# A first block ahead of the first states, a tick ahead of two scalings, and a sixth buffer, in a retention and Mish kernel on one core

## The chip, the core and the metric

The kernel runs on one core of a Trainium2 chip. The metric is the device time of one execution in microseconds (us); the times of several executions are given as a median with the lowest and the highest. Engines are named as in the profile: PE is TensorE, PEld its weight loads, DVE VectorE, ACT ScalarE, POOL GpSimd, SP SyncE (which only issues DMAs here).

## The reference

Batch 8, 8 heads, 576 positions, head size 64; the MLP has 512 columns and 2048 inner ones. In short:

```python
scores = q @ k.transpose(0, 1, 3, 2) / np.sqrt(64)
gamma  = 1 - 2.0 ** (-5 - np.arange(8))
rel    = pos[:, None] - pos[None, :]
ret    = scores * np.where(rel >= 0, gamma[:, None, None] ** rel, 0)   # causal decay, no softmax
x      = (ret @ v).transpose(0, 2, 1, 3).reshape(8 * 576, 512)
h      = x @ w_in                                                      # 4608 x 2048
out    = (h * np.tanh(log1p(exp(h)))) @ w_out                          # Mish, then 4608 x 512
```

## The kernel before

**Chunks and tiles.** The 4608 rows are cut into 36 chunks of 128. The first eight are the first 128 positions of the eight batches; the others hold positions 128 to 511 of each batch in three chunks, and the last 64 positions of two batches together. Four chunks make a tile of 512 rows, nine tiles in all (t = 0 to 8). For a tile, retention gives `xT` (512 columns by 512 rows), `g1(t, f)` makes block f of 16 of the inner layer (four 128x512 matmuls into one of two PSUM banks named hp, L568 or in halves L573, and a Mish activation on ACT into `gT`, L584), and the down projection multiplies `gT` by `w_out`.

**Retention in chunks.** A chunk's q and k are scaled on DVE (`step_p`, L341, two instructions, named P), its v by the decay (`step_v`, L348, named V: on DVE for chunks under 16, on POOL from 16 on). q and k are transposed (`step_t`: on PE for chunks under 16, by SP's DMA after that). A `visit(n)` for the pair n, n+1 adds the products of k and v of the next pair to the running states (L426), makes the outputs of its own pair from masked scores (L482) and from earlier states (L498), the scores of the next pair (L380), and after that DVE's mask product (`step_m`, L386). The scaled v of a chunk is in a buffer of the pool `tok`, which has five; a buffer is free when the matmuls of its chunk's visit have read it.

**The order.** The schedule is written by hand: every engine runs its instructions in the order in which the Python text gives them, and a semaphore wait holds up all that stands behind it on that engine. Three stretches of it matter here.

1. *Tile 0's down projection with tile 1's retention* (16 steps, `steps` at L860). Letters name tile 1's pieces: O is the output product of a batch's first chunk (`f_out`, its copy into `xT` at L251, half on DVE and half on ACT), F is `f_state` (L257, DVE), which scales v of one batch for the states that the first chunks leave. The down projection's four row blocks end in two hp banks, a bank ops and a bank st, and each is copied to `res` (L638) and stored by SP.
2. *Tile 1's sixteen blocks* (the loop over u at L893). `FIRST` places the first states in it: `first_states(of, what)` (L289, small matmuls, 64 rows and 64 columns) for tile `of`, row half `what`, into the banks st and ops; after the second half ACT copies both banks (L300). "turn" transposes tile 1's k (L264) and copies it, half on DVE and half on ACT (L270). `ps`, `vs` and `ts_` place the scalings and transposes of chunks 8 to 13.
3. *The later tiles* (the loop at L951), where n is the pair that is visited and w the step of eight in its half tile. In tile 2's second half (n = 14, i = 8 and 9) the loop asks for V of chunks 16 and 17. `tick` (L946) is a copy of one column of the newest `gT` block to `held` on POOL (L949), which makes POOL's queue wait for that activation; from i = 9 of tile 2 on it stands ahead of every load and every pair of scalings on POOL.

POOL also issues the loads of q, k and v (L325 and L329). At the visits of chunks 18, 20, 26, 30 and 32 the matmuls of the whole visit are in one step (w = 6), while V of the pair four chunks on is asked for at w = 3 (behind 32 there is none left).

Of the kernel before, what the change touches and what calls it, by code (L numbers as in the profile page):

```python
# [16 lines left out]
def kernel(  # L17
# [18 lines left out]
    nc = tc.nc  # L36
# [9 lines left out]
    NPE = 16  # L46
# [16 lines left out]
    wpool = ctx.enter_context(tc.tile_pool(name="weights", bufs=1))  # L63
    first = ctx.enter_context(tc.tile_pool(name="first", bufs=1))
    io = ctx.enter_context(tc.tile_pool(name="io", bufs=PF))
    tok = ctx.enter_context(tc.tile_pool(name="tok", bufs=5))
    tr = ctx.enter_context(tc.tile_pool(name="tr", bufs=4))
    xp = ctx.enter_context(tc.tile_pool(name="xp", bufs=2))
    gp = ctx.enter_context(tc.tile_pool(name="gp", bufs=2))
# [101 lines left out]
    def f_mix(g, i):  # L171

        name = ("qb", "kb")[i]
        fst[1][name, "mix", g] = room[3][:, ts(i, 1024)].rearrange("p (r x d) -> p r x d", r=8, x=2)
        nc.vector.tensor_copy(fst[1][name, "mix", g].rearrange("p r x d -> p x r d"),
                              fst[1][name][:, ds(2 * g, 2), :].rearrange("p x (r d) -> p x r d", r=8))
# [76 lines left out]
    def f_state(t, b, engine=nc.gpsimd):  # L253

        n = 4 * t + b
        v0s[n] = room[(6, 3)[t]][:, ts(b, H * D)].rearrange("p (h d) -> p h d", h=H)
        engine.tensor_tensor(v0s[n], v0[n], gv[:, 0, :].unsqueeze(2).to_broadcast([P, H, D]), op=OP.mult)  # L257

    def f_k0(t):

        tp = ps_sc.tile([P, 2, H, P], BF16, name="sc")
        for g in range(2):
            for h in range(H):
                nc.tensor.transpose(tp[:, g, h, :], fst[t]["kb", g][:, h, :], ident)  # L264
        return tp

    def f_k0_copy(t, tp, copies):
        for g in range(2):
            pair = first.tile([P, 2, H, D], BF16, name="k0", bufs=2)
            copies[g](pair.rearrange("p x h d -> p h x d"), tp[:, g].rearrange("p h (x d) -> p h x d", x=2))  # L270
            for x in range(2):
                k0[4 * t + 2 * g + x] = pair[:, x]
# [24 lines left out]
    def first_states_copy(t, copy):  # L297
        for i in range(2):
            pair = first.tile([P, 2, NP, 64], F32, name="s0", bufs=4)
            copy(pair, s0_banks[t][i])  # L300
            for x in range(2):
                s0[4 * t + 2 * i + x] = pair[:, x]
# [81 lines left out]
    def step_m(n):  # L384
        sm = tr.tile([P, 2, 2, NP, 64], BF16, name="sm", bufs=2)
        nc.vector.tensor_tensor(  # L386
            sm.rearrange("p e x n i -> p (e x n) i"), live[n]["sc"].rearrange("p e x n i -> p (e x n) i"),
            mask.unsqueeze(1).to_broadcast([P, 4 * NP, 64]), op=OP.mult)
        live[n]["sm"] = sm
# [405 lines left out]
    def att(n, steps):  # L795
        if n >= n_chunks:
            return
        for step in steps:
            {"P": step_p, "V": step_v, "T": step_t}[step](n)
# [57 lines left out]
        g1(0, f)  # L857
    for i in range(2):
        f_mix(0, i)
    steps = {0: "T0", 3: "S0 C1", 9: "T1", 11: "S1", 12: "V0 V1 V2 V3", 13: "F0 F1", 14: "O0 O1 O2 O3", 15: "F2 F3"}  # L860
    for i in range(nF):
        for step in steps.get(i, "").split():
            n = int(step[1])
# [25 lines left out]
    ps = {0: 0, 4: 1, 8: 2, 11: 3, 17: 5}  # L889
    vs = {0: 0, 5: 1, 9: 2, 13: 3, 18: 4, 19: 5}  # L890
    ts_ = {3: 0, 7: 1, 12: 2, 14: 3, 19: 4, 21: 5}
    FIRST = {0: (0, 0), 1: (1, 0), 2: ("turn", 1), 5: (0, 1), 6: (1, 1)}
    for u in range(24):  # L893
        j, w = divmod(u, 4)
        halved[0] = 2 if u < 1 else 0
        if u in FIRST:
            what, of = FIRST[u]
            if what == "turn":
                f_k0_copy(of, f_k0(of), (dve, act))
            else:  # L900
                first_states(of, what)
                if what:
                    first_states_copy(of, act)
        if u in ps:
            att(N0 + ps[u], "P")
        if u == 11:
            step_m(N0)
        if u in vs:
            att(N0 + vs[u], "V")
        if w == 0 and j > 0:  # L910
            if j < 5:
                load(N0 + j + 3)
            else:
                more_loads(N0 + j + PF)
        if u == 10:
            units = states(N0)
            units[0]()
            step_s(N0)
            units[1]()
            run(sums)  # L920
        elif u == 16:
            att(N0 + 4, "P")
            visit(N0, ((ps_o, "ops"), (ps_h, "hp")), (act, act))
            run(sums)
        elif u == 22:
            visit(N0 + 2, ((ps_h, "hp"), (ps_h, "hp")), (act, dve))
        if u == 20:
            stores(act)
        if u in (13, 20):
            run(casts, dve if u == 13 else act)  # L930
        if u in ts_:
            att(N0 + ts_[u], "T")
        stores()
        if u < nF:
            g1(1, u)
            flush()
        else:
            g2(1, u - nF)
# [7 lines left out]
    def tick(t, i):  # L946

        f = done.get(t, 0)
        nc.gpsimd.tensor_copy(held[:, i % 2:i % 2 + 1], gts[t][:, f, 0:1])  # L949

    for t in range(NS, nT):  # L951
        for i in range(nF):
            n, w = NCH * (t + 1) + i // 8 * 2, i % 8
            if w == (2 if t == NS else 0):
                run(casts, act)
            if t == NS and i == 0:
                halved[0] = 12
            for job in PLAN[i] if t > NS else ():
                if job[0] == "S":
                    g_sum(t - 1, int(job[1]))  # L960
            if t == NS:
                if w == 6:
                    visit(n, ((ps_h, "hp"), (ps_h, "hp")), (act, dve))
            elif n in WHOLE:
                if w == 6:
                    visit(n, ((ps_h, "hp"), (ps_h, "hp")), (act, act))
                elif w == 7:
                    run(sums)
            elif w == 2 and n < n_chunks:
                visit_first(n)  # L970
            elif w == 6 and n < n_chunks:
                visit_second(n, act)
            if w == 0:
                stores(act)
            if w == (3 if t > NS else 7 if n + 2 == NPE else 0) or w == 0 and n + 2 == NPE:
                run(sums)
            if w == 7 and n + 2 == NPE:
                stores(act)
            if w in (0, 1) and n + 2 < NPE:
                att(n + 2 + w, "P")  # L980
            if w == 1 and n + 4 == NPE:
                more_loads(n + 7)
            if w in ((4, 7) if n + 2 == NPE else (4, 5)) and n + 4 >= NPE:
                att(n + 4 + (w > 4), "P")
            if w in ((3, 4) if n + 2 < NPE else (0, 1)) and n <= NPE - 2:
                att(n + 2 + (w in (1, 4)), "V")
            if n + 2 >= NPE and w == (6 if n + 2 == NPE else 3) and n + 4 < n_chunks:
                tick(t, i)
                att(n + 4, "V")
                att(n + 5, "V")  # L990
            if t == NS and i in (3, 6, 10, 13):
                w_sum({3: 1, 6: 6, 10: 7, 13: 4}[i])

            if t == NS + 1 and i == 3:
                w_sum(3)
            if w == 7 and n + 4 == NPE:
                att(n + 5, "T")
            if w == (5 if n <= NPE - 2 else 7) and n + 4 >= NPE:
                att(n + 4, "T")
            if n + 2 >= NPE and w in PACED:  # L1000
                m, part = ((0, 2), (1, 2), (0, 0), (0, 1), (1, 0), (1, 1))[PACED.index(w)]
                if n + 6 + m < n_chunks:
                    tick(t, i)
                    load_part(n + 6 + m, part)
            if w == 5 and n + 4 < NPE:
                more_loads(n + w + 2)
            if w in (4, 5) and n + 2 < NPE:
                att(n - 2 + w, "T")
            if w == 0 and n == NPE or w == 7 and n >= NPE:
                att(n + (3 if w == 0 else 5), "T")  # L1010
            stores(act)


            if t == 2:
                if w == 6:
                    g2(1, 8 + i // 2)
                g1(t, i)
                if i % 2 and w != 7:
                    g2(1, 8 + i // 2)
            else:  # L1020
                if i == 15:
                    rest()
                jobs = (PLAN if n < n_chunks else ALONE)[i]
                for job in reversed(jobs) if n in WHOLE and w == 6 else jobs:
                    if job[0] == "g":
                        g1(t, int(job[1:]))
                    elif job[0] == "U":
                        unit(t - 1, int(job[1:]))
                if i == 8:
                    rest()  # L1030
# [31 lines left out]
```

## Time and profile before

| what | value |
|---|---|
| median of 3 runs | 294.47 us (294.01 to 295.0) |
| the profiled execution, its span | 293.21 us, 291.5 us |
| granted TensorE clock | 1.0 |
| busy time: PE, DVE, ACT, POOL | 282.3, 189.4, 155.3, 151.4 us |
| HBM | 36.70 MB read, 9.44 MB written, 158 GB/s over the span |

The profile is of one execution. Its times start at the span's start. A line such as `54.39 1.03 PE L568 MATMUL ... x4` of the timeline gives the start, the duration, the engine, the line of the kernel, the operation with its tiles and shapes, and how many were merged; brackets give the idle time of the engine before it and what ended that. A line of the waits gives who waited for whom, for how long in total, how often, and the longest.

### The profile page before, as it was taken

To read this page: it belongs to the slowest core of one execution; us is meant where nothing else is said; L and a number is where in the kernel's file an instruction comes from. 1 tells how busy PE (TensorE), PEld (TensorE's weight loads), DVE (VectorE), ACT (ScalarE), POOL (GpSimd) and SP (SyncE) were. 2 spreads that over 40 slices of the span, in tenths; PEclk is the share of its full clock that TensorE was granted. 3 is DMA by queue.
4 is the path that set the end of the run, shared out by engine and by line. 5 is a ranking of instruction groups with operands and counts; after the bars stand their busy time and mean duration, and the time that the engine had idled before them with its cause. 6 is when DMAs were issued, how large, how long until landed. Compare 5 with 4: busy or idle time off the path is not lost.

```text
span 291.5 us, 8716 instructions
## 1 busy us (share of the span) xinstructions
PE 282.3 (97%) x3788; PEld 186.2 (64%) x3788; DVE 189.4 (65%) x273; ACT 155.3 (53%) x269; POOL 151.4 (52%) x225
## 2 busy tenths in 40 slices
PE   7899999999998999999999999999999999999994
PEld 3566786555664556666756766666666766665783
DVE  4842449739699399786588767966786173523383
ACT  5656324876674564755464646554656556444320
POOL 8695842688792977567379875777430000000000
PEclk9999999999999999999999999999999999999999
DMA  7999999987999995959696996499826001201033
GB/s 156 206 206 205 205 237 231 290 210 161 236 261 176 162 199 122 179 157 168 197 187 177 187 236 159 146 179 218 183 86 127 12 2 73 74 0 72 22 104 94
DMA packets 41543, 45.91 MB, mean 158 GB/s; under 512 B 23841, under 2 KB 31265, under 8 KB 41505
## 3 DMA queue, kind: packets, MB, share of 16 engines
q0 software_dynamic: 14256, 30.15, 49.5%
q1 hardware_dynamic: 26656, 14.69, 24.0%
q8 instruction: 29, 0.48, 0.7%
q10 hardware_dynamic: 592, 0.52, 0.6%
q14 instruction: 10, 0.07, 0.1%
HBM read 36.70 MB, written 9.44 MB: 158 GB/s over the span
## 4 chain that ended last, share of the span: by engine, by line
PE 84%; DVE 6%; DMA 5%; POOL 2%; issue 1%; ACT 1%; POOLq 0%; ACTq 0%
PE hp L568 38%; PE ops L680 26%; PE hp L573 5%; DMA gT<-in_v_dram 3%; DVE qks L341 2%; DMA qkraw<-in_k_dram 2%; PE hp L680 2%; PE ops L568 2%; PE sc L426 2%; PE sc L380 1%; PE sc L759 1%; POOL gT L107 1%; PE ops L573 1%; PE st L573 1%; DVE sm L386 1%
## 5 line engine op out<-in xcount | busy, mean ns | idle before, releaser
L568 PE MATMUL hp<-xT,w_in_t 128*128 128x512 bf16 x534 | 129.9, 379 | 0.2 <-ACT gT L584 0.2
L584 ACT ACTIVATE gT<-hp 128x512 bf16<-128x512 f32 x144 | 86.1, 600 | 60.6 <-PE hp L568 58.5
L568 PEld LDWEIGHTS <-w_in_t 128*128 128x128 bf16 x534 | 50.9, 98 | 47.5 <-issue 1.6
L680 PEld LDWEIGHTS <-room 128*128 128x128 bf16 x528 | 51.3, 98 | 13.6 <-issue 0.8
L341 DVE TENSOR_TENSOR qks<-qkraw,gqk 128x512 bf16<-128x512 f32 x56 | 45.0, 854 | 4.9 <-issue 4.0
L671 DVE TENSOR_TENSOR room<-gT 128x2048 bf16<-128x2048 bf16 x35 | 42.2, 1229 | 0.8 <-ACT gT L584 0.8
L680 PE MATMUL ops<-room,room 128*128 128x256 bf16 x304 | 37.5, 273 | 0.5 <-ACT res L710 0.5
L949 POOL COPY held<-gT 128x1 bf16<-128x1 bf16 x57 | 19.4, 340 | 29.0 <-ACT gT L584 28.9
L348 POOL TENSOR_TENSOR vs<-vraw,gv 128x512 bf16<-128x512 f32 x20 | 26.2, 1319 | 11.7 <-PE hp L482 11.7
L386 DVE TENSOR_TENSOR sm<-sc,mask 128x1024 bf16<-128x1024 f32 x14 | 17.1, 1221 | 17.5 <-PE sc L380 10.8
L680 PEld LDWEIGHTS <-gT 128*128 128x128 bf16 x224 | 21.7, 98 | 6.2 <-issue 0.2
L680 PE MATMUL ops<-w_out_t,room 128*128 128x256 bf16 x192 | 22.9, 273 | 0.0
L325 POOL DMA_DIRECT2D vraw<-in_v_dram x24 | 21.3, 887 | 2.6 <-DMA w_out_t<-in_moe_w_out_dram 1.4
L325 POOL DMA_DIRECT2D qkraw<-in_q_dram x24 | 21.7, 904 | 1.7 <-issue 1.3
L325 POOL DMA_DIRECT2D qkraw<-in_k_dram x24 | 21.2, 883 | 0.0
L450 DVE TENSOR_TENSOR total<-sc,total 128x256 f32<-128x256 f32 x32 | 13.5, 423 | 3.6 <-PE sc L426 2.8
L680 PE MATMUL ops<-room,gT 128*128 128x256 bf16 x112 | 13.4, 273 | 0.0
L573 PEld LDWEIGHTS <-gT 128*128 128x128 bf16 x120 | 11.6, 98 | 2.4
L573 PE MATMUL hp<-xT,w_in_t 128*128 128x256 bf16 x84 | 12.6, 273 | 0.0
L680 PE MATMUL ops<-w_out_t,gT 128*128 128x256 bf16 x96 | 12.3, 273 | 0.0
L568 PE MATMUL ops<-w_out_t,gT 128*128 128x512 bf16 x46 | 12.1, 380 | 0.0
L712 DVE TENSOR_TENSOR res<-ops,res 128x512 f32<-128x512 f32 x6 | 4.2, 692 | 12.1 <-PE ops L680 12.1
(156 smaller groups left out, 348.6 us busy)
## 6 DMA issues: line engine op xcount, KB each, us to landing
out_dram<-res SPq DMA_DIRECT2D x29, 256.0 KB, 4.1
qkraw<-in_q_dram POOLq DMA_DIRECT2D x24, 256.0 KB, 6.0
qkraw<-in_k_dram POOLq DMA_DIRECT2D x24, 256.0 KB, 6.7
vraw<-in_v_dram POOLq DMA_DIRECT2D x24, 256.0 KB, 6.6
w_out_t<-in_moe_w_out_dram POOLq DMA_DIRECT2D x4, 512.0 KB, 11.1
w_in_t<-in_moe_w_in_dram POOLq DMA_DIRECT2D x3, 512.0 KB, 9.6
out_dram<-res SPq DMA_DIRECT2D x9, 128.0 KB, 2.5
gT<-in_k_dram POOLq DMA_DIRECT2D x8, 128.0 KB, 6.5
```

What stands on the lines that cost most here:

```text
L325: nc.gpsimd.dma_start(out=t, in_=src[b, :, ds(P * c, P), :].rearrange("h p d -> p h d"))
L341: nc.vector.tensor_tensor(slots[:, :, y], heads[:, :, y], factors[:, :, y].unsqueeze(3).to_broadcast([P, NP, 2, D]), op=OP.mult)
L348: engine.tensor_tensor(vs, live[n]["v"], gv[:, c, :].unsqueeze(2).to_broadcast([P, H, D]), op=OP.mult)
L386: nc.vector.tensor_tensor(sm.rearrange("p e x n i -> p (e x n) i"), live[n]["sc"].rearrange("p e x n i -> p (e x n) i"), mask.unsqueeze(1) ...
L426: nc.tensor.matmul(st[ds(64 * e, 64), j, x, p, :], lhsT=ks, rhs=vs, start=True, stop=True, skip_group_check=True)
L450: nc.vector.tensor_tensor(new[:, k], st[:, j, x], total[b], op=OP.add)
L568: nc.tensor.matmul(to, lhsT=w, rhs=x, start=first, stop=last)
L573: nc.tensor.matmul(to[:, ts(j, n)], lhsT=w, rhs=x[:, ts(j, n)], start=False, stop=False, skip_group_check=True)
L584: nc.scalar.activation(gts[t][:, f, :], hp, AX.Mish)
L671: engine.tensor_tensor(to, g_half(t, *a), g_half(t, *b), op=op_)
L680: nc.tensor.matmul(bank[:, half, :], lhsT=g[:, f, ts(half, P)], rhs=w[:, f, :], start=(f == 0 and half == 0 and not add), stop=(f == hF - ...
L949: nc.gpsimd.tensor_copy(held[:, i % 2:i % 2 + 1], gts[t][:, f, 0:1])
```

## The change

Three edits, in one file:

- In the u loop the first states of tile 0 and the turn of tile 1's k each move one step back (u = 1, 2, 3 in place of 0, 1, 2), so that block 0 of tile 1 stands first. The scalings F0 and F1 move from step 13 to step 15 of the stretch before, behind the O steps; F2 and F3 move from step 15 to u = 1 and u = 2, called directly.
- At tile 2, i = 8, a `tick` is put ahead of V of chunks 16 and 17. `done` is then 7: it is the block with index 7 of tile 2.
- The pool `tok` gets six buffers in place of five.

PE and DVE run the same instructions as before in another order, POOL one copy more; ACT runs the same as well, and SP's order is as before.

```diff
-    tok = ctx.enter_context(tc.tile_pool(name="tok", bufs=5))
+    tok = ctx.enter_context(tc.tile_pool(name="tok", bufs=6))
...
-    steps = {0: "T0", 3: "S0 C1", 9: "T1", 11: "S1", 12: "V0 V1 V2 V3", 13: "F0 F1", 14: "O0 O1 O2 O3", 15: "F2 F3"}
+    steps = {0: "T0", 3: "S0 C1", 9: "T1", 11: "S1", 12: "V0 V1 V2 V3", 14: "O0 O1 O2 O3", 15: "F0 F1"}
...
-    FIRST = {0: (0, 0), 1: (1, 0), 2: ("turn", 1), 5: (0, 1), 6: (1, 1)}
+    FIRST = {1: (0, 0), 2: (1, 0), 3: ("turn", 1), 5: (0, 1), 6: (1, 1)}
...
         if u in vs:
             att(N0 + vs[u], "V")
+        if u in (1, 2):
+            f_state(1, u + 1, nc.vector)
...
+            if w == 0 and n + 2 == NPE:
+                tick(t, i)
             if w in ((3, 4) if n + 2 < NPE else (0, 1)) and n <= NPE - 2:
                 att(n + 2 + (w in (1, 4)), "V")
```

## The prediction

> **What bounds the kernel now.** I read the page's busy table first, then TensorE's list of waits, then its timeline around each wait, then the timelines of VectorE, ScalarE and GpSimd at the same places.
>
> The page's first part:
> ```profile
> PE 282.3 (97%) x3788; PEld 186.2 (64%) x3788; DVE 189.4 (65%) x273; ACT 155.3 (53%) x269; POOL 151.4 (52%) x225
> ```
> TensorE (PE) is the bound, so only what makes PE wait can pay. The clock row is 9 in all forty slices. PE's waits (waited for: total, times, longest, in us):
> ```profile
> PE sc L426 <- DVE vs L348: 0.8, 1, 0.8
> PE st L289 <- ACT res L638: 0.7, 1, 0.7
> ...
> PE ops L680 <- ACT res L710: 0.5, 1, 0.5
> ...
> PE hp L568 <- ACT gT L584: 0.2, 1, 0.2
> ```
> Behind the first 17 us these four are all: no other entry lies there. In PE's timeline (start, duration, line, tiles, count, idle before):
> ```profile
> 48.48 0.38 PE L568 MATMUL st<-w_out_t,gT 128*128 128x512 bf16 x1
> 49.54 0.22 PE L289 MATMUL st<-room,k 64*64 64x64 bf16 x2 [0.68 <-ACT res L638]
> ...
> 54.39 1.03 PE L568 MATMUL hp<-xT,w_in_t 128*128 128x512 bf16 x4
> 55.57 1.02 PE L568 MATMUL hp<-xT,w_in_t 128*128 128x512 bf16 x4 [0.15 <-ACT gT L584]
> ...
> 87.27 1.03 PE L568 MATMUL ops<-w_out_t,gT 128*128 128x512 bf16 x4
> 89.05 0.32 PE L426 MATMUL sc<-vs,qks 64*64 64x64 bf16 x16 [0.75 <-DVE vs L348]
> ```
> Ends of matmuls are modelled, so I count starts. Eight 128x512 matmuls start 1.73 us apart from the next group (62.89 to 64.62), 0.216 each. The matmul of 48.48 is done with its turn at 48.70 and the next starts at 49.54: **stall A, 0.84 us**. In the same way 54.39 + 0.86 = 55.25, next at 55.57: **stall B, 0.32**. And 87.27 + 0.86 = 88.13, next at 89.05: **stall C, 0.92**. Without a wait, a change to the 64-row matmuls leaves 0.09 (50.62 + 0.22 = 50.84, next 50.93).
>
> Stall A is the first states: they write the banks st and ops, in which the first tile's last two row blocks lie until ScalarE (48.90 to 49.49) and VectorE (48.85 to 49.53) have copied them out. Stall C is the visit of chunk 12, which needs the scaled v of chunk 15. VectorE and GpSimd there:
> ```profile
> 85.42 1.53 DVE L341 TENSOR_TENSOR qks<-qkraw,gqk 128x512 bf16<-128x512 f32 x1
> 86.87 1.53 DVE L341 TENSOR_TENSOR qks<-qkraw,gqk 128x512 bf16<-128x512 f32 x1
> 88.32 0.68 DVE L348 TENSOR_TENSOR vs<-vraw,gv 128x512 bf16<-128x512 f32 x1
> ```
> ```profile
> 86.36 1.48 POOL L348 TENSOR_TENSOR vs<-vraw,gv 128x512 bf16<-128x512 f32 x1
> 89.61 1.50 POOL L348 TENSOR_TENSOR vs<-vraw,gv 128x512 bf16<-128x512 f32 x1 [1.76 <-PE hp L482]
> ```
> A scaling at L341 has a median of 0.68; these two take 1.53 each, the second while GpSimd scales v of chunk 16 (86.36). The 1.70 that they lose is what makes chunk 15's v late.
>
> **First edit, the block ahead of the states.** The same instructions run; only their order changes. PE goes from 48.70 straight into block 0 of tile 1. Its input xT must be there: ScalarE's half ends at 48.07; VectorE's half, today 47.72 to 48.94 behind two scalings (1.28), moves ahead of them and runs about 46.60 to 47.82. The two hp banks were copied out by 46.63. So the block fills 48.70 to 49.57 and hides the copies (VectorE's now 48.05 to 48.73, as its source ends at 47.99; ScalarE's unchanged to 49.49). The states follow at 49.66 with the 0.09 change: A falls from 0.84 to 0.09, gain 0.75.
>
> What is late next? The transposes of k (0.90) now end at 53.19, block 3 runs 53.64 to 54.50, block 4 to 55.36, the states of tile 1's row half to 55.87. ScalarE runs behind: VectorE's k copy 53.39 to 54.08, ScalarE's k copy (1.01, which today too starts when VectorE's ends) to 55.1, half a qkT copy (0.59, overlapping) to 55.6, block 3's activation to about 56.1. Block 5 needs that activation's bank, so it waits from 55.87 to about 56.15: stall B moves from block 4 to block 5 at nearly its size. Gain 0; bounds +0.32 (gone) and -0.7 (one more 1.01 copy ahead of the activation, less the 0.3 already counted). I take 0, because it is the same queue with the same copies.
>
> The four scalings of tile 1's v for the states (0.60 apart, 2.4 in all) move behind the xT copy; the last two end near 52.9, and VectorE has 0.74 idle today ahead of the k copy, so nothing waits for them. SP's queue keeps its order: the marker between the two row halves of the states stands behind two stores and is due at 50.95, as today at 50.93. No DMA moves.
>
> **Second edit, the tick ahead of chunks 16 and 17.** One more 128x1 copy on GpSimd (0.19 to 1.25 in the rows of L949) waits for block 7 of tile 2, whose activation starts at 93.13 and ends at 93.73. Both scalings, today at 86.36 and 89.61, then start near 94. Chunk 16's key scaling on VectorE falls from 2.98 to about 1.28, chunk 15's v is ready at 87.3, ahead of PE at 88.13: C falls from 0.92 to 0.09, gain 0.83. Only the second of the slowed scalings lies beside GpSimd's scaling in the rows; if the first one's 0.85 is something else, v is ready at 88.15, and the gain is still about 0.8. The other inputs of that visit are there: the last transposed chunk is copied by 87.77, block 5's bank is free at 88.25.
>
> Behind the waiting tick GpSimd holds the two scalings and the loads that today start at 95.29. The scalings take 1.04 (alone) to 1.50 (beside VectorE), so they end at 96.1 to 97.6; the next visit needs them at 100.79, 3 us later. The loads start 1.3 to 3 us later; the last of their group today is issued about 104.7, takes 4.5 to 5.7 to land, and is read behind 112.14 + 1.3. There is cover of 1 to 3 us; without it VectorE would be late by the rest, with the mask product of 116.66 behind it. I count nothing.
>
> **Third edit, the sixth buffer.** It removes no PE wait: PE waits for no scaled v but at C. It removes GpSimd's waits:
> ```profile
> its engine sat idle before it (us, times) until:
>   PE hp L482: 11.7, 5
> ```
> One is the 1.76 above; the rest are at the visits of chunks 18, 20, 26 and 30 (2.25, 3.76, 1.71, 2.25). There the second scaling of a pair will run right behind the first, beside VectorE's four key scalings, and the loads go out earlier by as much. Where two run together today (112.23) VectorE's four take 4.18, where one does 3.34 (125.63): 0.84 more. VectorE's idle time ahead of the next mask product is 1.06, 1.35, 0.51 and 1.04, so only the third is short, by 0.33, and 1.08 of idle follows there. I count 0.
>
> The Trainium skill, "SBUF — State Buffer", section "Who interferes with whom", speaks against this edit: a VectorE instruction with two SBUF inputs and a GpSimd one that reads SBUF shut each other out, the later one standing still for a whole instruction. By it a meeting costs a whole scaling, 1.04 in place of 0.84; then two more of the four idle times (1.06, 1.04) are used up to within 0.02 and the third is short by 0.53. The sum would stay, but I would give the third rival below 0.15 in place of 0.11.
>
> **Sum.** 0.75 + 0 + 0.83 = 1.58. The profiled execution took 293.21 (span 291.5, 1.7 around it): 291.6. It lies 1.26 under the median of 294.47, from which the same 1.6 gives **292.9**. All stages behind 90 us are PE-bound, with loads gated by activations, so the gain is carried to the end; the stall of 0.70 at 151.21 hangs on a chain that starts from PE and stays.
>
> **The rivals.** (1) *Only one stall goes.* Either ScalarE's queue makes B grow by what A gives (bound -0.7 above), or chunk 15's v still comes late. For: both have under 0.4 us of slack in my working. Against: each slack is positive. Time: 294.47 - 0.8 = 293.7.
> (2) *Nothing is left.* PE is at 97%, and both gains turn into waits further on, VectorE being held by landings: it waited 0.91 for one at 56.68. Against: chunk 17's key load, issued at 79.34 with a median of 6.1 to land, is there by 85.5, and VectorE wants it at 86.4 even when 0.8 early. Time: 294.5.
> (3) *Slower, by the sixth buffer.* At the four visits GpSimd holds VectorE for two scalings in a row. The longest key scaling in the rows is 2.09, 1.41 over the usual; two of these are 2.82, against 0.85 counted today, so 1.97 more at each, past the idle times by 0.91, 0.62, 1.46 and 0.93, 3.9 in all. If mask products and the copies behind them passed all of it on to PE: 294.47 - 1.6 + 3.9 = 296.8. It decides from 0.6 of PE loss per visit. Against: 2.09 is a single row, and 1.1 of idle follows behind most of these products.
>
> **How the numbers follow.** About 0.3% (0.9 us) is what a measurement of this kernel can tell from no change. Both stalls gone: 0.63, between 292.2 and 293.4 with B's bounds. Rival 1: 0.17, within 0.3%, though a part of it (0.03) reaches past. Rival 2: 0.09. Rival 3, with other ways to lose: 0.11. So faster 0.66, same 0.23, slower 0.11. The range takes in the first two and most of rival 2, down to B gone and the run's own spread of 0.5: 292.0 to 294.3.
>
> **What would show it.** Right: PE goes from the last st matmul to an hp matmul 0.22 later; no wait of L289 for L638; a wait of some 0.3 at block 5 in place of block 4; L426 waits no longer for L348; chunk 16's two key scalings take about 0.7 each (one may be 1.5); GpSimd's scalings stand behind a tick at about 92, with no wait for L482 anywhere. Wrong: a new PE wait of over 0.5 us behind ScalarE's k copy, at the visits of chunks 14, 18, 20, 26 or 30, or a wait of VectorE for a landing ahead of one of these.

## The result, and the profile after

The changed kernel takes 292.5 us (median; 291.89 to 292.89) against 294.47 (294.01 to 295.0), five executions of each: a ratio of 0.9935 with a 95% interval of 0.9916 to 0.9954, or 1.9 us less (1.35 to 2.5). A second measurement, made with the last experiments, gave 0.9927 (0.9908 to 0.9946). The forecast was 292.9. Comparisons leave out executions that took over 1.5% more than the fastest of the same kernel, and two profiles of such executions (303.6 us, the first edit alone; 297.4, the changed kernel with five buffers), which have further PE waits from 100 us on, are read up to 95 us only.

The profiled execution has a span of 290.7, only 0.8 less than before. The rest is lost at its start, where PE waits longer for first loads: 1.4 for q, against 0.6 before (the first line below), and 0.5 for the first weights, against nothing. So what stood at 48.48 before stands at 49.39. PE's list of waits (waited for: total, times, longest), the kernel before and then the changed one:
```profile
PE st L193 <- DMA gT<-in_q_dram: 0.6, 1, 0.6
```
```profile
PE st L193 <- DMA gT<-in_q_dram: 1.4, 2, 0.8
PE ops L164 <- DVE room L126: 1.3, 1, 1.3
PE ops L680 <- ACT res L710: 0.5, 1, 0.5
PE hp L568 <- DMA w_in_t<-in_moe_w_in_dram: 0.5, 1, 0.5
...
PE hp L568 <- ACT gT L584: 0.3, 1, 0.3
```
The waits for L638 (stall A) and for L348 (stall C) are gone; behind 22 us only L710 and L584 are left. So times are compared from the last st matmul of L568 on. PE's timeline at the places of the prediction:
```profile
49.39 0.38 PE L568 MATMUL st<-w_out_t,gT 128*128 128x512 bf16 x1
49.60 0.38 PE L568 MATMUL hp<-xT,w_in_t 128*128 128x512 bf16 x1
...
50.57 0.22 PE L289 MATMUL st<-room,k 64*64 64x64 bf16 x2
...
57.04 1.02 PE L568 MATMUL hp<-xT,w_in_t 128*128 128x512 bf16 x4 [0.27 <-ACT gT L584]
...
59.24 0.61 PE L360 MATMUL sc<-ident,qks 128*128 128x128 bf16 x8
...
87.40 1.03 PE L568 MATMUL ops<-w_out_t,gT 128*128 128x512 bf16 x4
88.36 0.32 PE L426 MATMUL sc<-vs,qks 64*64 64x64 bf16 x16
...
150.48 1.03 PE L680 MATMUL ops<-room,room 128*128 128x256 bf16 x8 [0.54 <-ACT res L710]
```
From the last st matmul to four landmarks:

| landmark | before | after | less |
|---|---|---|---|
| chunk 9's transposes (59.12, 59.24) | 10.64 | 9.85 | 0.79 |
| the visit of chunk 12 (89.05, 88.36) | 40.57 | 38.97 | 1.60 |
| the wait for L710 (151.21, 150.48) | 102.73 | 101.09 | 1.64 |
| end of the span (291.5, 290.7) | 243.0 | 241.3 | 1.7 |

The gain is made in two places, 0.79 and 0.81, and carried to the end. VectorE and GpSimd at the second one:
```profile
85.54 1.29 DVE L341 TENSOR_TENSOR qks<-qkraw,gqk 128x512 bf16<-128x512 f32 x2
86.74 0.69 DVE L348 TENSOR_TENSOR vs<-vraw,gv 128x512 bf16<-128x512 f32 x1
```
```profile
85.86 0.88 POOL L325 DMA_DIRECT2D vraw<-in_v_dram  x1
93.07 0.19 POOL L951 COPY held<-gT 128x1 bf16<-128x1 bf16 x1 [6.32 <-ACT gT L584]
93.21 3.02 POOL L348 TENSOR_TENSOR vs<-vraw,gv 128x512 bf16<-128x512 f32 x2
```
Chunk 16's two key scalings take 1.29 in place of 2.98, although GpSimd issues a load beside them; its own scalings stand behind the tick.

### The profile page after: what moved, and what is told of

The parts are those of the page before. It is cut to its first block, busy times and chain, and to the rows that moved or that the text cites. A ratio compares the mean times of both kernels' runs of the same rounds, so it can differ in the third digit from the quotient of the medians.

```text
span 290.7 us, 8717 instructions
## 1 busy us (share of the span) xinstructions
PE 281.9 (97%) x3788; PEld 186.2 (64%) x3788; DVE 193.1 (66%) x273; ACT 155.7 (54%) x269; POOL 156.0 (54%) x226
## 4 chain that ended last, share of the span: by engine, by line
PE 88%; DMA 4%; POOL 3%; DVE 2%; ACT 1%; issue 1%; POOLq 0%; ACTq 0%
PE hp L568 39%; PE ops L680 26%; PE hp L573 5%; DMA w_in_t<-in_moe_w_in_dram 4%; PE ops L568 4%; PE hp L680 2%; PE sc L426 2%; PE sc L380 2%; PE ops L573 1%; PE sc L759 1%; POOL gT L107 1%; PE st L573 1%; POOL gT L118 1%; PE hp L498 1%; PE sc L360 1%
## 5 line engine op out<-in xcount | busy, mean ns | idle before, releaser
L568 PE MATMUL hp<-xT,w_in_t 128*128 128x512 bf16 x534 | 129.9, 379 | 0.8 <-DMA w_in_t<-in_moe_w_in_dram 0.5
L584 ACT ACTIVATE gT<-hp 128x512 bf16<-128x512 f32 x144 | 86.2, 601 | 60.3 <-PE hp L568 59.0
L568 PEld LDWEIGHTS <-w_in_t 128*128 128x128 bf16 x534 | 51.0, 98 | 48.2 <-issue 1.2
L680 PEld LDWEIGHTS <-room 128*128 128x128 bf16 x528 | 51.3, 98 | 13.6 <-issue 0.8
L341 DVE TENSOR_TENSOR qks<-qkraw,gqk 128x512 bf16<-128x512 f32 x56 | 48.6, 917 | 3.6 <-issue 2.8
L951 POOL COPY held<-gT 128x1 bf16<-128x1 bf16 x58 | 23.2, 400 | 33.7 <-ACT gT L584 33.6
L680 PE MATMUL ops<-room,room 128*128 128x256 bf16 x304 | 37.5, 273 | 0.5 <-ACT res L710 0.5
L348 POOL TENSOR_TENSOR vs<-vraw,gv 128x512 bf16<-128x512 f32 x20 | 26.9, 1364 | 0.0
L680 PEld LDWEIGHTS <-gT 128*128 128x128 bf16 x224 | 21.7, 98 | 6.2 <-issue 0.2
L325 POOL DMA_DIRECT2D vraw<-in_v_dram x24 | 21.9, 912 | 2.5 <-DMA w_out_t<-in_moe_w_out_dram 1.3
L325 POOL DMA_DIRECT2D qkraw<-in_q_dram x24 | 22.3, 929 | 1.2 <-DVE xT L510 0.6
L680 PE MATMUL ops<-w_out_t,room 128*128 128x256 bf16 x192 | 22.9, 273 | 0.0
L325 POOL DMA_DIRECT2D qkraw<-in_k_dram x24 | 21.8, 909 | 0.0
L680 PE MATMUL ops<-room,gT 128*128 128x256 bf16 x112 | 13.4, 273 | 0.0
L680 PE MATMUL ops<-w_out_t,gT 128*128 128x256 bf16 x96 | 12.3, 273 | 0.0
L568 PE MATMUL ops<-w_out_t,gT 128*128 128x512 bf16 x46 | 12.1, 380 | 0.0
```

The source lines that it names most:

```text
L325: nc.gpsimd.dma_start(out=t, in_=src[b, :, ds(P * c, P), :].rearrange("h p d -> p h d"))
L341: nc.vector.tensor_tensor(slots[:, :, y], heads[:, :, y], factors[:, :, y].unsqueeze(3).to_broadcast([P, NP, 2, D]), op=OP.mult)
L348: engine.tensor_tensor(vs, live[n]["v"], gv[:, c, :].unsqueeze(2).to_broadcast([P, H, D]), op=OP.mult)
L568: nc.tensor.matmul(to, lhsT=w, rhs=x, start=first, stop=last)
L584: nc.scalar.activation(gts[t][:, f, :], hp, AX.Mish)
L680: nc.tensor.matmul(bank[:, half, :], lhsT=g[:, f, ts(half, P)], rhs=w[:, f, :], start=(f == 0 and half == 0 and not add), stop=(f == hF - ...
```

## The experiments

The theory: A and C are separate stalls, each worth its length; the order edit removes A, the tick removes C by taking GpSimd's scalings from beside VectorE's, and the sixth buffer removes no PE wait. Rivals: one gain is lost again; the key scalings are slowed by loads, not by GpSimd's scaling; the buffer carries a part.

**The first edit alone.**
```diff
-    steps = {..., 12: "V0 V1 V2 V3", 13: "F0 F1", 14: "O0 O1 O2 O3", 15: "F2 F3"}
+    steps = {..., 12: "V0 V1 V2 V3", 14: "O0 O1 O2 O3", 15: "F0 F1"}
...
-    FIRST = {0: (0, 0), 1: (1, 0), 2: ("turn", 1), ...}
+    FIRST = {1: (0, 0), 2: (1, 0), 3: ("turn", 1), ...}
...
+        if u in (1, 2):
+            f_state(1, u + 1, nc.vector)
```


> The kernel before with the first edit alone (block 0 of tile 1 ahead of the first states, the four scalings behind). Theory (each stall has its own cause, gains add up): stall A falls from 0.84 to 0.09 us, stall B moves from block 4 to block 5 with 0.3 to 0.4, so PE is 0.75 to 0.8 earlier at the transposes behind block 6, and the time falls by 0.8. Stall C (0.92 before) should shrink by itself, because VectorE is 0.8 earlier against GpSimd, whose loads keep their time: chunk 15's v then meets at most one of GpSimd's scalings (0.85 late), which leaves C between 0.1 and 0.9 and the time 0.8 to 1.6 under the kernel before. Rival (one gain of two is lost): no more than 0.3 gained, with a new wait behind ScalarE's k copy.

Measured: 0.9967 (0.9947 to 0.9987), about 1.0 less: at the lower end of the theory, above the rival's 0.3. Stall B moved to block 5 (0.27). C was not there in this profile, but its loads ran late (GpSimd's scaling at 88.84), so that told little. A second profile settled it.

**The first edit alone, a profile to be read to its end.** The same kernel.

> The first edit alone once more, for a profile that can be read to its end. Theory (place decides): the start of GpSimd's scaling of chunk 16 against VectorE's scaling of chunk 15's v sets stall C. If it starts while VectorE still has chunk 16's keys or chunk 15's v ahead (before about 87 us on PE's clock of the changed kernel), C is 0.1 to 0.9; if GpSimd's loads run later than that, C is 0.09 and only A's gain and C's are both there. Rival (C is closed by the first edit whatever GpSimd does): no wait for L348 and scalings of chunk 15's v at 0.68 although GpSimd's scaling overlaps it.

Measured: span 291.0. VectorE, GpSimd and PE's wait:
```profile
84.57 2.13 DVE L341 TENSOR_TENSOR qks<-qkraw,gqk 128x512 bf16<-128x512 f32 x2
86.63 0.68 DVE L348 TENSOR_TENSOR vs<-vraw,gv 128x512 bf16<-128x512 f32 x1
87.23 3.13 DVE L341 TENSOR_TENSOR qks<-qkraw,gqk 128x512 bf16<-128x512 f32 x2
```
```profile
86.72 2.49 POOL L348 TENSOR_TENSOR vs<-vraw,gv 128x512 bf16<-128x512 f32 x2
```
```profile
PE hp L568 <- DVE xT L510: 0.5, 1, 0.5
```
C is closed: chunk 15's v started 0.09 ahead of GpSimd's scaling and ran at 0.68. The expectation counts on the clock of the changed kernel, where all this lies 0.97 later (chunk 9's transposes are at 58.27 here, at 59.24 there): GpSimd's scaling then starts at 87.69, behind 87, which is the theory's second case. For C that case came true. That both gains are then there did not: GpSimd's two scalings met chunk 17's keys (3.13 for two), VectorE's copy to xT behind them was late, and PE waited for its hp bank, 0.70 by starts. The rival's sign, 0.68 beside an overlapping scaling, is there too, but VectorE had started first; that the first edit closes C whatever GpSimd does is ruled out further on, by the kernel without the tick. So the first edit alone only moves the stall from the visit to block 7: it keeps A's gain and, at the wait for L710, 0.20 of C's 0.81.

**The tick alone.**
```diff
+            if w == 0 and n + 2 == NPE:
+                tick(t, i)
```


> The kernel before with the tick alone, five buffers. Theory: stalls A and B stay (0.84 and 0.32), C falls from 0.92 to 0.09, the two key scalings of chunk 16 take 1.28 together instead of 2.98, time lower by 0.8. Rival (the key scalings are slowed by the loads that GpSimd issues, not by its scaling): they stay at 2 us or more and C at 0.5 or more, gain under 0.4.

Measured: 0.9968 (0.9952 to 0.9985), 0.9 less. VectorE, GpSimd, and a wait of PE that no other profile has:
```profile
86.57 1.29 DVE L341 TENSOR_TENSOR qks<-qkraw,gqk 128x512 bf16<-128x512 f32 x2
```
```profile
85.96 0.88 POOL L325 DMA_DIRECT2D vraw<-in_v_dram  x1
```
```profile
PE st L289 <- SPq L411: 0.8, 1, 0.8
```
The two key scalings take 1.29 together, L426 waits for nothing, A and B are there. That is the theory's number, and the rival with the loads falls: a load is still issued beside them. The wait of 0.8 for SP's marker, at 52.09, stands behind two stores whose issue took SP 2.11 here and 0.82 before. It lies ahead of chunk 9's transposes; counted from these, the visit of chunk 12 comes 0.81 sooner than before and the end 0.85.

**The sixth buffer alone.**
```diff
-    tok = ctx.enter_context(tc.tile_pool(name="tok", bufs=5))
+    tok = ctx.enter_context(tc.tile_pool(name="tok", bufs=6))
```


> The kernel before with the sixth buffer alone. Theory (GpSimd's scaling shuts out VectorE's for 0.85 each): v of chunk 17 no longer waits for the visit of chunk 12, runs right behind that of chunk 16 (from about 87.9) and delays chunk 15's v on VectorE once more, so stall C grows from 0.92 to about 1.8 and the time rises by 0.8, to 295.3. Rival (the buffer only takes waits off GpSimd): C stays at 0.9, time within 0.3 of the kernel before.

Measured: 295.46 against 294.23, ratio 1.004 (1.0019 to 1.006): slower by 1.2, with 0.8 expected. VectorE, GpSimd, PE's wait:
```profile
85.92 3.99 DVE L341 TENSOR_TENSOR qks<-qkraw,gqk 128x512 bf16<-128x512 f32 x2
89.83 0.68 DVE L348 TENSOR_TENSOR vs<-vraw,gv 128x512 bf16<-128x512 f32 x1
```
```profile
86.81 2.55 POOL L348 TENSOR_TENSOR vs<-vraw,gv 128x512 bf16<-128x512 f32 x2
```
```profile
PE sc L426 <- DVE vs L348: 1.8, 1, 1.8
```
The wait that the old buffer count imposed on chunk 17's v was holding it away from VectorE. Without it GpSimd runs both scalings on end, VectorE's two take 3.99 (1.53 and 2.53), and C grows from 0.75 to 1.75 idle: the theory's way, by 1.00 where it counted 0.85. The profile holds one more wait that the kernel before does not have, 0.7 ahead of L482 at 110.92, in the middle of a group of matmuls; what ended it is not shown, so nothing is read from it.

**The changed kernel with five buffers.** The edit is the last one's, undone in the changed kernel.

> The changed kernel with five buffers for scaled v in place of six. Theory (the buffer removes no PE wait): the same time as the changed kernel, 292.5 within 0.4; GpSimd's waits for L482 come back at the visits of chunks 18, 20, 26 and 30, some 10 us in all, and PE's waits are the same three. Rival (the buffer carries a part of the gain, by loads that go out 2 to 4 us earlier): slower than the changed kernel by 0.4 or more, with a PE or VectorE wait behind one of these visits.

Measured: 0.993 (0.9914 to 0.9945), the changed kernel's ratio. GpSimd's waits are back; the profile of the last experiment, which has five buffers too, shows them (what GpSimd sat idle for ahead of scaled v: total, times):
```profile
  PE hp L482: 9.5, 4
```
They cost nothing that can be measured. The buffer is neutral where the tick stands and harmful where it does not.

**The changed kernel without the tick.** The tick's two lines are taken out, six buffers stay.

> The changed kernel without the tick, six buffers kept. Theory (place decides: GpSimd's two scalings run as soon as its loads are issued, and each shuts VectorE out for 0.85): with PE and VectorE 0.8 earlier than in the kernel before, they start near 86.8 beside chunk 15's v instead of ahead of it, so stall C comes back with 0.1 to 1.0, and the time is 0.1 to 1.0 over the changed kernel; it is under 1.75, the wait of the kernel with the sixth buffer alone. Rival (first edit alone closes C): no wait for L348, same time as the changed kernel.

Measured: 0.9979 (0.996 to 0.9998), so about 1.3 over the changed kernel's 0.9935, past the expected 1.0; in the profiles, from block 0 of tile 1 to the end, it is 0.85.
```profile
87.94 1.52 DVE L348 TENSOR_TENSOR vs<-vraw,gv 128x512 bf16<-128x512 f32 x1
```
```profile
87.62 1.29 POOL L348 TENSOR_TENSOR vs<-vraw,gv 128x512 bf16<-128x512 f32 x1
```
```profile
PE sc L426 <- DVE vs L348: 0.7, 1, 0.7
```
Here GpSimd started first (87.62 against 87.94) and chunk 15's v took 1.52; with the first edit alone VectorE started first (86.63 against 86.72) and it took 0.68. A difference of 0.4 us in who starts first decides whether C is there. Without the tick that hangs on when the loads were issued, as far as these profiles go; the tick takes it out of chance.

**Both halves of the k copy on VectorE.**
```diff
-                f_k0_copy(of, f_k0(of), (dve, act))
+                f_k0_copy(of, f_k0(of), (dve, dve))
```


> The changed kernel with both halves of tile 1's k copy on VectorE. Theory (what is left of stall B, 0.42 us by starts at block 5, hangs on ScalarE's queue: k copy 1.01 ahead of block 3's activation): block 3's activation ends 0.5 or more earlier, the wait at block 5 goes, 0.33 less; with the noise of a median the time lies 0 to 0.6 under the changed kernel. Rival (VectorE's queue takes it over, by the scalings of chunk 9 that stand behind): the same wait reappears at the states behind block 4 or at chunk 9's transposes, and nothing is gained.

Measured: 0.9933 (0.9908 to 0.9957). In the profile the wait at block 5 is gone and nothing took its place (from block 0 of tile 1 to chunk 9's transposes PE takes 9.32 in place of 9.64); in the times 0.3 cannot be told from nothing.

**The cast behind the bank copy.**
```diff
-            if w == (2 if t == NS else 0):
+            if w == (2 if t == NS else 0) and (t, i) != (NS + 2, 8):
                 run(casts, act)
...
                         unit(t - 1, int(job[1:]))
+                        if (t, i) == (NS + 2, 8):
+                            run(casts, act)
```


> The changed kernel with one cast of state sums on ScalarE (tile 4, step 8) put behind the bank copy of L710 in place of ahead of it. Theory (the stall of 0.70 at about 150.5, PE waiting for L710, is that copy standing behind a cast that waits for VectorE's sums): the wait for L710 goes, 0.6 less, and nothing replaces it, since the states are read 1 us after the cast. Rival (the cast is then late for the visit of chunk 22, or the activation behind it is): the wait moves to L498 or L568 at nearly its size and the time is that of the changed kernel.

Measured: 0.991 (0.9889 to 0.9931). ScalarE's timeline in the changed kernel, then in this one:
```profile
148.59 1.05 ACT L457 CAST ssb<-total 128x1024 bf16<-128x1024 f32 x1 [0.62 <-DVE total L450]
...
149.85 0.58 ACT L710 COPY res<-ops 128x512 f32<-128x512 f32 x1
```
```profile
147.62 0.59 ACT L710 COPY res<-ops 128x512 f32<-128x512 f32 x1 [0.28 <-PE ops L680]
148.10 1.05 ACT L457 CAST ssb<-total 128x1024 bf16<-128x1024 f32 x1
```
The cast no longer holds up the bank copy, and the wait for L710 is gone. But 0.3 of its 0.7 is given back at 270 us: ScalarE's copy of a bank at L716, which in the changed kernel ends just as PE wants the bank (271.66 for 271.69), ends at 270.63 here, 0.3 late for PE, whose next matmul at L680 starts at 270.68 in place of 270.36. Why that copy did not move up with PE is not shown.

**Both, with six buffers and with five.**

> The changed kernel with both edits of the two runs above, the k copy on VectorE and the cast behind the bank copy. Theory (each PE wait is worth its own length wherever it lies): 0.9 less than the changed kernel, about 291.5 against a kernel before of 294.3, ratio 0.990. Rival (gains at one place are given back later): no better than the better one of the two.

> The changed kernel once more, beside the next one on the same chip. Expected as before: ratio 0.993 to 0.994 to the kernel before, PE waits behind 17 us only at block 5 (0.3) and for L710 (0.5).

> The changed kernel with the k copy on VectorE, the cast behind the bank copy, and five buffers. Theory (waits are worth their length, the sixth buffer nothing): 0.9 less than the changed kernel in the same call, ratio 0.990 to 0.991; no PE wait behind 17 us of over 0.2; GpSimd's waits for L482 of some 10 us are back at no cost. Rival (the buffer matters once the other waits are gone): within 0.3 of the changed kernel.

Measured: with six buffers 0.9907 (0.9883 to 0.9931) with a median of 291.42; with five 0.9931 (0.9908 to 0.9954) with a median of 291.72, beside the changed kernel once more at 0.9927 and 292.06. Behind 17 us neither profile has a PE wait over 0.2, and the spans are 289.5 and 289.3 against 290.7 and 290.6. From the start of tile 1's block 0 to the end of the span it is 241.1 in both profiles of the changed kernel, 240.9 with the k copy on VectorE, 240.7 with the cast behind, 240.4 and 240.5 with both edits. So the two edits add up, but to 0.7 in place of the expected 0.9, for the 0.3 given back at 270 us. The medians lie 0.3 to 1.1 lower than the changed kernel's, but the intervals overlap, and the ratio with five buffers is no lower than the changed kernel's beside it: that these versions beat it is shown by the traces and not by the times.

## Why the prediction was right, point by point

- **Stall A.** Forecast 0.84 to 0.09, gain 0.75. The hp matmul follows the st matmul after 0.21; A and B together give 0.79.
- **Stall B.** Forecast to move from block 4 to block 5, waiting from 55.87 to 56.15. It did, with 0.27, for the reason given: ScalarE's k copy on VectorE removed it.
- **Stall C.** Forecast gain 0.83; measured 0.81 (40.57 - 38.97 - 0.79). The doubt about the first key scaling's 0.85 is answered: both run at the usual length, so the whole 1.70 went with the tick.
- **The tick's queue.** GpSimd's scalings took 3.02, their upper bound, and the next load went out at 96.77 instead of 95.29, at the early end of the forecast 1.3 to 3 us. No PE wait came of it, as counted.
- **The sixth buffer.** Forecast 0, with the third of the four visits short by 0.33. At that visit VectorE's timeline shows it, before and after:
```profile
184.04 3.89 DVE L341 TENSOR_TENSOR qks<-qkraw,gqk 128x512 bf16<-128x512 f32 x4
188.44 1.23 DVE L386 TENSOR_TENSOR sm<-sc,mask 128x1024 bf16<-128x1024 f32 x1 [0.51 <-PE hp L498]
...
192.13 0.69 DVE L719 TENSOR_TENSOR res<-res,ops 128x512 f32<-128x512 f32 x1 [1.08 <-PE ops L680]
```
```profile
183.31 4.89 DVE L341 TENSOR_TENSOR qks<-qkraw,gqk 128x512 bf16<-128x512 f32 x4
188.12 1.21 DVE L386 TENSOR_TENSOR sm<-sc,mask 128x1024 bf16<-128x1024 f32 x1
...
191.41 0.69 DVE L719 TENSOR_TENSOR res<-res,ops 128x512 f32<-128x512 f32 x1 [0.68 <-PE ops L680]
```
  GpSimd's second scaling cost the key scalings 1.00 here (4.89 for 3.89), not the 0.84 that the prediction took from 4.18 and 3.34. So the shortage was 0.49 in place of 0.33: the mask product has no idle time left ahead of it, and the 1.08 ahead of L719 fell to 0.68, 0.40 late, and absorbed. VectorE's time at L341 rose from 45.0 to 48.6 in all. What the prediction missed is that the buffer alone would have been slower; it counted the edits as independent where this one needs the tick.
- **The rivals.** Of the first, only the mechanism was seen, and only with edits left out: with the order edit alone C's stall turns up at block 7. The second did not come, VectorE was not held by landings ahead of a PE wait. The third, slower by the buffer, has its mechanism at chunks 16 and 17, not at the four visits where the prediction put it.
- **The size.** Forecast 1.6 less; 1.7 in the trace, 1.9 (1.35 to 2.5) in the times. The difference is within the noise of the medians.

The Trainium skill, "SBUF — State Buffer", section "Who interferes with whom", says that whichever of the two engines starts first holds the other off. The pair 86.63 against 86.72 and 87.94 against 87.62 agrees. By its price, a whole instruction of the other, a scaling of GpSimd's costs VectorE 1.04. The traces show both less and about that: where each of VectorE's scalings met one of GpSimd's, it mostly lost 0.84 or 0.85; where one of VectorE's met two in a row, the second cost 1.00 (2.53 for 1.53 with the buffer alone and with the first edit alone, 3.09 for 2.09 at the third visit).

## What to carry to other kernels

When two queues share something, look at who starts first at the one instruction that the bound engine waits for, and pin that order with a wait that costs nothing, instead of leaving it to load times. A wait that looks like pure idle time may be what keeps two engines apart: before taking it away (a buffer more), see what will run in its place, and test each edit alone and each one left out. A stall that is removed is worth its length only as far as nothing behind it catches up: compare at landmarks, up to the end. A first instruction stalled on banks that are being copied out is cheaply covered by a block that needs other banks, and the stall that comes next is found in the copying engine's queue.

## What the runs showed of the hardware that was not expected

Where GpSimd's scaling stands directly behind a load, VectorE lost 0.85 once more in four profiles, and before the scaling's recorded start: one of the two scalings of chunk 16's keys took 1.53 in the kernel before (85.42, GpSimd's scaling at 86.36), the first of them took 1.53 with the buffer alone (85.92, scaling at 86.81), and the pair took 2.13 with the first edit alone (84.57, scaling at 86.72) and without the tick (85.89, scaling at 87.62). In the other profile of the first edit alone a key scaling lost only 0.26 (87.23, scaling at 88.84). With the tick ahead, the pair ran at 1.29 beside the same loads. The cause stays open; the recorded starts of GpSimd may be late, which no run here tests.
